# Linear attention and a gated MLP on one core: products from raw turned x with centred weights, queries token by token

## The chip, the cores and the metric

The kernel runs on one NeuronCore of a Trainium2 chip. The metric is device microseconds of one execution. The core has five engines, each with a queue of its own that it works through in order: TensorE (PE in the profile; its weight loads are shown as PEld), VectorE (DVE), ScalarE (ACT), GpSimd (POOL) and SyncE (SP), which here does nothing but issue DMAs. [...]

## The reference

A pre-norm layer on x of 2048 tokens by 448, in bfloat16: linear attention of 16 heads of 28 with softmax feature maps, then an MLP with a gate.

```python
def _layernorm(x): return (x - mean(x)) / sqrt(var(x) + 1e-5)

def _A_ref(x, wqkv, w_phi, wo):
    q, k, v = split((x @ wqkv), heads=16)             # 28 each
    pq, pk = q @ w_phi[h], k @ w_phi[h]
    phi_q = concat([softmax(pq), softmax(-pq)])       # 56 features
    phi_k = concat([softmax(pk), softmax(-pk)])
    kv = einsum("bhsf,bhsd->bhfd", phi_k, v)
    z  = sum over s of phi_k
    o  = (phi_q @ kv) / (phi_q . z + 1e-6)
    return o @ wo

def _B_ref(x, w_gate, w_up, w_down):
    return (sigmoid(x @ w_gate) * (x @ w_up)) @ w_down

h  = x + _A_ref(_layernorm(x), ...)
h2 = h + _B_ref(_layernorm(h), ...)
```

## The kernel before

Tokens are worked in 16 tiles of 128 (t = 0 to 15), in four chunks of 512 (c = 0 to 3). A contraction over 448 rows is done in seven steps of 64 rows, two of them at a time on the upper and lower half of TensorE's array (`pair`, `both`; all such matmuls have the helper's line, L311). The names below are those of the program's operations; each engine's order of them is written out by hand in `ORDER`, and `Graph.emit` adds semaphore waits where one operation needs another's data or buffer. `PROGRAM` lists the stages behind the key and value stage.

Start: x, key, value and query weights are loaded (`x0`.., `ld_k`, `ld_v`, `ld_q`; `ld_q` are transposing DMAs). `w_phi` is spread into block-diagonal form (`wsp`, `wex`), the key weights are turned on TensorE (`wT0` to `wT3`, copied by `wTe`), and key and query weights are multiplied with it (`fold`: `w2m0_k` for the keys, `w2m1_k` for the queries, copied by `w2e`), so that pk and pq are one product from normalized x. `warm0` to `warm9` are matmuls of zeros between these steps. Meanwhile VectorE takes mean and variance of each tile (`bst`, `agg`), GpSimd the power -1/2 (`pow1`), and `xn` writes normalized x. Tiles 0 to 3 are turned on TensorE (`xT0` to `xT3`, `xTe`), tiles 4 to 15 by transposing DMAs (`xT4` to `xT15`, L585) that SP issues as each `xn` is done.

Keys and values, per tile: `ppa/ppb` and `vva/vvb` (two tiles at a time, first four tiles) or `pva/pvb` make pk and v in PSUM; ScalarE takes exp of pk and of -pk (`ek`, L673 and L674) and copies v (`v1`); VectorE sums the exponentials per head (`ss`, L677) and inverts (`rs`); GpSimd or VectorE multiplies (`phi`, L687); TensorE adds phi-transposed times v onto the state in PSUM banks 6 and 7 (`kva`, `kvb`). The state is masked to its heads' blocks in four pieces (`kvzA` to `kvzD`).

Queries, per chunk and half of the heads (`pqa`, `pqb`; eight pairs): the folded query weights are the stationary operand, normalized x the moving one of 512 columns, so pq comes out turned, features on partitions. ScalarE takes exp of it and of its negative (`eq`, L723). These stand as they are for the numerators (`num`, per tile), for which VectorE does the divisions (`rsm qq b c rden`); `o` normalizes, then `oT` turns the result (tiles 0 and 1 on TensorE, others by DMA, L825), `woa/wob` project it. `h` adds x, `sq nm ve pow2` give the second layer norm's numbers, `hn` normalizes, `hT` turns it (tiles 0 and 1 on TensorE, others by DMA, L861). Then per 128 hidden rows `ga/gb` make gate and up, `sig` and `hh` combine them, `dn/dp/dm` project down, `fin` adds and `out` stores.

Of the kernel before, what the change touches and what calls it, by code (L numbers as in the profile page):

```python
# [1021 lines left out]
```

## Time and profile before

| | before |
|---|---|
| median of 3 runs | 204.06 us (203.86 to 204.12) |
| the profiled execution | 203.73 us |
| its span, first to last instruction | 201.9 us |
| busy: PE, DVE, ACT, POOL | 196.3, 132.3, 92.5, 56.5 us |
| DMA moved | 16.27 MB, 32491 packets |
| HBM read, written | 8.34 MB, 1.84 MB |

A row of a group of instructions gives line, engine, operation, what it writes and reads by the program's names, shape and count, then the group's busy time in us and the mean of one in ns, then the engine's idle time before them with what ended it. A row of the timeline or of the chain begins with start and length in us. SPq is SP's sequencer issuing a DMA. A row with x and a slashed triple gives the shortest, middle and longest of one in ns.

### The profile page before, as it was taken

Reading aid. Unit: us, or ns where it says so; the run is one execution under the profiler, and the core shown is the slowest. Engines: PE = TensorE matmul, PEld = TensorE weight load, DVE = VectorE, ACT = ScalarE, POOL = GpSimd, SP = SyncE. Lnnn points to the kernel's source line nnn. Section 1 sums busy time; section 2 is a strip of 40 time slices with the busy share of each in tenths; the row PEclk is TensorE's granted clock in tenths of the full one; section 3 lists DMA queues with packets and bytes.
Section 4 is the critical chain, followed back from the end, with each engine's and each line's share of the span. In section 5 each row is a group of like instructions: output and inputs, shape, how many; then the busy total and the mean of one; then the engine's idle time right before and its main releaser. Section 6 shows DMA issues by size and latency. Waiting matters only on the chain.

```text
span 201.9 us, 5885 instructions
## 1 busy us (share of the span) xinstructions
PE 196.3 (97%) x2516; PEld 114.0 (56%) x2516; DVE 132.3 (65%) x319; ACT 92.5 (46%) x191; POOL 56.5 (28%) x95
## 2 busy tenths in 40 slices
PE   7999999999989999999999999999999999999995
PEld 4835656665558778676444444555555555554443
DVE  4899999978899677767758977436432422272224
ACT  3768998899772636222333342324422212222220
POOL 6579949533433613600042020001400000000000
PEclk9999999999999999999999999999999999999999
DMA  6956444839983320251005411030312000004002
GB/s 155 281 133 159 67 83 78 246 132 269 317 197 75 65 43 3 52 81 29 0 3 123 81 26 26 4 74 28 66 38 52 0 3 0 0 3 136 0 3 91
DMA packets 32491, 16.27 MB, mean 81 GB/s; under 512 B 24720, under 2 KB 31568, under 8 KB 32464
## 3 DMA queue, kind: packets, MB, share of 16 engines
q1 hardware_dynamic: 32336, 15.86, 32.4%
q8 instruction: 20, 0.33, 0.7%
q14 instruction: 7, 0.06, 0.1%
q10 hardware_dynamic: 128, 0.03, 0.1%
HBM read 8.34 MB, written 1.84 MB: 50 GB/s over the span
## 4 chain that ended last, share of the span: by engine, by line
PE 91%; DVE 4%; DMA 2%; SPq 1%; issue 1%; POOL 1%
PE psum L311 84%; PE psum L943 5%; DMA x_sb<-in_A_x_dram 2%; SPq L415 1%; DVE st L547 1%; PE psum L540 1%; DVE st L831 1%; POOL rst L835 1%; PE psum L614 0%; DVE hn_pad L853 0%; DVE xnT L533 0%; DVE b_sb L803 0%; DVE Wk L533 0%; DVE c_sb L806 0%; DVE rsm L800 0%
## 5 line engine op out<-in xcount | busy, mean ns | idle before, releaser
L311 PE MATMUL psum<-xnT,wg_sb 64*128 64x512 bf16 (+1 forms) x490 | 93.1, 333 | 0.2
L311 PE MATMUL psum<-xnT,wu_sb 64*128 64x512 bf16 (+1 forms) x490 | 92.9, 333 | 0.0
L915 ACT ACTIVATE sg_sb<-psum 128x512 bf16<-128x512 f32 (+1 forms) x70 | 34.8, 511 | 91.3 <-PE psum L311 90.8
L916 DVE SCALAR_TENSOR_TENSOR hhT<-sg_sb,psum 128x512 bf16<-128x512 bf16 (+1 forms) x70 | 38.9, 576 | 54.4 <-ACT sg_sb L915 54.2
L311 PEld LDWEIGHTS psum<-xnT,wg_sb 64*128 64x128 bf16 x490 | 44.4, 94 | 22.5 <-DVE hhT L916 4.2
L311 PEld LDWEIGHTS psum<-xnT,wu_sb 64*128 64x128 bf16 x490 | 44.4, 94 | 13.0
L311 PE MATMUL psum<-wd_sb,hhT 64*128 64x448 bf16 x336 | 36.9, 349 | 0.0
L311 PEld LDWEIGHTS psum<-wd_sb,hhT 64*128 64x128 bf16 x336 | 17.6, 94 | 14.4 <-DVE x_sb L838 0.5
L311 PE MATMUL psum<-wv_sb,xnT 64*128 64x448 bf16 x112 | 22.3, 351 | 0.1
L311 PE MATMUL psum<-Wk,xnT 64*128 64x448 bf16 x112 | 22.1, 350 | 0.2
L847 POOL TENSOR_SCALAR ve<-ssq 128x1 f32<-128x1 f32 x11 | 2.2, 201 | 55.0 <-ACT junk L844 54.8
L677 DVE TENSOR_REDUCE ss<-hhT 128x32 f32<-128x896 bf16 x16 | 16.6, 1052 | 0.3 <-ACT hhT L674 0.2
L723 ACT ACTIVATE eq<-psum 120x1024 bf16<-120x1024 f32 x16 | 15.7, 1024 | 1.0 <-PE psum L311 0.8
L687 POOL TENSOR_TENSOR phi<-hhT,rs 128x896 bf16<-128x896 bf16 x8 | 13.7, 1718 | 6.0 <-DVE rs L683 3.6
L311 PE MATMUL psum<-xnT,Wq 64*120 64x512 bf16 x112 | 15.0, 384 | 0.1
L812 POOL TENSOR_TENSOR o_pad<-c_sb,rden 128x448 bf16<-128x448 bf16 x10 | 9.3, 935 | 14.9 <-DVE rden L808 14.8
L311 PE MATMUL psum<-wo_o,oT 64*128 64x448 bf16 x56 | 13.2, 349 | 0.0
L311 PE MATMUL psum<-wo_e,oT 64*128 64x448 bf16 x56 | 13.1, 349 | 0.0
L943 PE MATMUL psum<-wd_sb,hhT 128*128 128x448 bf16 (+2 forms) x70 | 11.2, 316 | 0.0
L950 DVE SCALAR_TENSOR_TENSOR x_sb<-psum,x_sb 128x448 bf16<-128x448 f32 (+2 forms) x17 | 9.4, 592 | 2.7 <-PE psum L943 1.6
L311 PEld LDWEIGHTS psum<-Wk,xnT 64*128 64x128 bf16 x112 | 7.7, 94 | 5.6 <-PE psum L311 1.0
L803 DVE TENSOR_TENSOR b_sb<-psum,qq 128x464 bf16<-128x464 f32 x16 | 10.2, 636 | 0.7 <-PE psum L311 0.4
(105 smaller groups left out, 235.6 us busy)
## 6 DMA issues: line engine op xcount, KB each, us to landing
out_dram<-x_sb SPq DMA_DIRECT2D x15, 112.0 KB, 1.8
x_sb<-in_A_x_dram SPq DMA_DIRECT2D x7, 224.0 KB, 4.0
wd_sb<-in_B_w_down_dram SPq DMA_DIRECT2D x7, 224.0 KB, 4.5
wg_sb<-in_B_w_gate_dram SPq DMA_DIRECT2D x3, 448.0 KB, 6.3
wu_sb<-in_B_w_up_dram SPq DMA_DIRECT2D x3, 448.0 KB, 6.2
wv_sb<-in_A_wqkv_dram SPq DMA_DIRECT2D x2, 224.0 KB, 4.0
wk_sb<-in_A_wqkv_dram SPq DMA_DIRECT2D x2, 196.0 KB, 3.3
wo_e<-in_A_wo_dram SPq DMA_DIRECT2D x1, 336.0 KB, 3.3
```

The source lines that it names most:

```text
L311: p = e.matmul(o, lhsT=w, rhs=r, start=st, stop=sp, tile_position=(row, 0))
L415: return op(eng, name, lambda e: e.dma_start(dst, src), r=r, w=w, dma="in" if eng == "sp" else "ain", nring=48 if eng == "sp" else 8, kb=kb)
L677: op("dve", "ss%d" % t, lambda e: e.tensor_reduce(ss[:, s, :].rearrange("p (b h) -> p b h", h=2), eks.rearrange("p b (d h) -> p b h d", h= ...
L687: return e.tensor_tensor(phi[:, sp, :, :, :].rearrange("p b a n -> p (b a) n")[:, :, 0:56].rearrange("p b (d h) -> p b d h", h=2), eks.rea ...
L723: op("act", "eq%d_%d%s" % (c, i, "pm"[sg]), lambda e, sg=sg: e.activation(eq[c][:, sg, 2 * i:2 * i + 2, :].rearrange("p g n -> p (g n)"), ...
L803: op("dve", "b%d" % t, lambda e: e.tensor_tensor(h3(b_sb), OMv[:, :, :, 0:EV], h2(qq)[:, :, :, None].to_broadcast([P, NB, 8, EV]), ALU.mul ...
L812: return e.tensor_tensor(o_pad[:, t % NO, off:off + D].rearrange("p (h d) -> p h d", h=H), c_sb[:, t % NS, :, 0:DH], rden[:, t % NS, :][:, ...
L847: op(("pool", "dve"), "ve%d" % t, lambda e: e.tensor_scalar(ve2[:, t:t + 1], ssq2[:, t:t + 1], 1.0 / D ** 3, EPS, op0=ALU.mult, op1=ALU.ad ...
L915: op("act", "sig" + nm, lambda e: e.activation(sg_sb[:, k, 0:N], bk(bg)[:, 0:N], ACT.Tanh, scale=0.5), r=[B(bg)], w=[("sg", k)])
L916: op("dve", "hh" + nm, lambda e: e.scalar_tensor_tensor(out=hhT[(t0 // 4) % NHH][:, ff, ns], in0=sg_sb[:, k, 0:N], scalar=1.0, in1=bk(bu)[ ...
L943: p = e.matmul(bk(b)[:, lo:hi], lhsT=hb[:, ff, TS(t)], rhs=wd_sb[:, ff, lo:hi], start=ff == 0, stop=ff == FT - 1)
L950: op("dve", "fin%d%s" % (t, nm), lambda e: e.scalar_tensor_tensor(out=h_sb[:, t, lo:hi], in0=bk(b)[:, lo:hi], scalar=0.5, in1=h_sb[:, t, l ...
```

## The change

Products are made from x as it is loaded. For the mean, the weights are centred: the mean over the 448 rows is taken out of the value weights (`vms` sums by ones on TensorE, `vme` scales, `vc0` and `vc2` add) and of the folded query weights (`qms qme qc0 qc2`); for the keys it is got from a column of ones in the turning matmuls (`identk`, `ksum`, `kmean`) and added by four more matmuls per block (`w2c0` to `w2c3`). The deviation is put in as the scale of the exponentials (`rst1`, and `nrst1` for the negative) and of the `v1` copies. `xn` and the query half of the old layout go. Tiles 0 to 3 of raw x are turned on TensorE (`rT0` to `rT3`), the others two at a time by a transposing DMA of eight 128x128 blocks (`rT4` to `rT14`), for which x is loaded in two overlapping windows (`x_pad`).

Queries are made per tile like keys (448 columns, tokens on partitions, `pqa`, `pqb` for two tiles), their exponentials (`eq0` to `eq15`) go into one of five buffers `eqs`, and one transposing DMA of 16 blocks per two tiles (`eT0` to `eT14`) turns them. Four of the five buffers lie in the MLP's `hhT`, so some `hh` wait for an `eT`. The state's mask is two operations on all partitions (`kvzA`, `kvzB`). h lies where weights lay. All five orders are written anew.

```diff
 ORDER sp:
-x1 x0 ld_k0 ld_k2 x2 x4 ld_v2 x8 x6 ld_q2 ld_q1 ld_v0 x10 ld_q0 ld_q3 xT4 x12 x14 xT5 ... xT15 ld_woe0 ld_woe1
-ld_woo0 ld_woo1 ld_wg0 ld_wu0 ... ld_wu3 ld_wd0 ld_wd1 ld_wd2 oT2 oT3 ld_wd3 ... ld_wd6 oT4 oT5 oT6 oT7 hT2 hT3 oT8 ...
+ld_k2 ld_k0 x0 x4a x4b ld_v2 x1 x2 ld_v0 x6a x6b x10a x10b ld_q2 rT4 ld_q0 ld_q1 ld_q3 ld_woo0 rT8 ld_woe0
+ld_woe1 rT6 ld_woo1 ld_wg3 ld_wd6 ld_wd0 rT10 ld_wd1 ld_wu2 rT12 rT14 ld_wu3 ld_wg2 ld_wd4 ld_wg0 ld_wu1 eT0
+ld_wd3 ld_wu0 eT2 eT4 ld_wg1 eT6 ld_wd5 eT8 oT3 oT2 ld_wd2 eT12 oT4 oT5 oT6 oT7 eT10 hT2 hT3 hT4 eT14 hT5 oT8 ...
 ORDER pe (the start, and from the end of the state on):
-warm0 warm1 warm2 wsp warm3 wT0 wT1 warm4 wT2 wT3 warm5 w2m0_0 w2m0_1 w2m0_2 warm6 w2m0_3 xT1 xT0 warm7 warm8 warm9 xT3 ppa0 ...
+warm0 wsp wT3 wT0 wT2 wT1 warm1 rT1 rT0 w2m0_2 w2m0_3 w2m0_1 w2c2 w2c3 w2c1 rT2 w2m0_0 w2c0 vms rT3 ppa0 ppb0 vva0 ...
-kva15 kvb15 qs pqa1_1 num0 pqb1_1 num1 pqa2_0 num2 pqb2_0 pqa2_1 oT0 oT1 num3 pqb2_1 woa0 wob0 num4 pqa3_0 pqb3_0 wgu
-pqa3_1 num5 pqb3_1 hT1 hT0 num6 ga0_1 ga0_0 gb0_1 gb0_0 woa2 num7 ga0_2 ga0_3 gb0_2 gb0_3 wob2 num8 ga0_4 ga0_5 ... woa4 ...
+kva15 kvb15 qs pqa6 num0 num1 pqb6 pqa8 pqb8 num2 pqa10 oT0 oT1 pqb10 num3 woa0 pqa12 wob0 pqb12 num4 pqa14 pqb14 hT0 hT1
+num5 ga0_1 ga0_0 gb0_1 gb0_0 num6 woa2 ga0_2 ga0_3 gb0_2 wob2 gb0_3 ga0_4 num7 gb0_4 ga0_5 gb0_5 woa4 ...
 ORDER dve:
-... xn0 ... xn2 ... xn11 ... xn12 ... xn14 ...; phi1 3 5 6 11 12 14 15; ... b4 c4 hn0 hn1 rsm5 qq5 b5 hT1e c5 hT0e ...
+... agg3 vc0 vc2 nr1_0 bst7 bst9 agg7 agg2 ss0 ...; phi5 6 9 14 15; ... b4 hn0 hn1 c4 hT0e hT1e rsm5 ...
 ORDER act:
+... v1_10 ek10 eq0 ek11 v1_11 ek12 v1_12 eq1 ek13 ek14 v1_14 ek15 v1_15 eq2 eq3 eq4 ... eq8 oT1e eq9 ... eq12 h0 h1 eq14 eq13 eq15 sig0_1
...
-        def xnorm(t, a): ...
+        def raw(t):
+            if t < NV2:
+                pe_transpose("rT%d" % t, [x_sb[:, t, r0:r0 + P] for r0 in ROW0], 6 + t % 2, xrT[t], ("x", t), ("xr", t))
+            elif t % 2 == 0:
+                dst = hnT[t // 4][:, t % 4:t % 4 + 2, :].rearrange("p t n -> p (t n)").rearrange("p (k n) -> p k n", n=P)
+                src = x_pad[:, t - NV2:t - NV2 + 2, :].rearrange("p t n -> p (t n)")
+                op("sp", "rT%d" % t, lambda e: e.dma_start_transpose(out=dst, in_=src), ...)
...
+        op("dve", "ksum", ... tensor_reduce of the ones' columns ..., r=[B(i) for i in range(6)] + [("WkT", k) for k in range(KT)])
+        def centre(nm, w, key, b, j):
+            def mean(e):
+                for i, (k, h) in enumerate(((0, slice(0, P)), (1, slice(0, P)), (2, HI), (3, slice(0, P)))):
+                    p = e.matmul(bk(b)[:, 0:D], lhsT=ones[h, :], rhs=w[h, k, :], start=i == 0, stop=i == 3)
+                return p
+            op("pe", nm + "ms", mean, ...)
+            op(("act", "dve"), nm + "me", ... mul by -1.0 / D into junk ...)
+            for k in (0, 2):
+                op(("dve", "pool"), "%sc%d" % (nm, k), lambda e, k=k: e.tensor_tensor(w[:, k:k + 2, :], w[:, k:k + 2, :],
+                                                     junk[:, j, None, :].to_broadcast([P, 2, D]), ALU.add), ...)
...
             def ekf(e):
-                e.activation(ek[:, s, :, 0, :], src, ACT.Exp)
-                return e.activation(ek[:, s, :, 1, :], src, ACT.Exp, scale=-1.0)
+                e.activation(ek[:, s, :, 0, :], src, ACT.Exp, scale=rst1[:, t:t + 1])
+                return e.activation(ek[:, s, :, 1, :], src, ACT.Exp, scale=nrst1[:, t:t + 1])
...
         def pq(c, i, b):
-            f1, f2 = pair(bk(b)[:GR, :], bk(b + 1)[:GR, :], lambda h, k: W2[1][h, k, 2 * i, 0:GR], ..., lambda h, k: xnT[c][h, k, :], ...)
-            for sg in range(2):
-                op("act", "eq%d_%d%s" % (c, i, "pm"[sg]), ... Exp of 120x1024, scale=1.0 - 2.0 * sg ...)
+            t = 4 * c + 2 * i
+            proj2("pq", t, b, wq2, W2q)
+            s = eq_at[t // 2]
+            for u in (t, t + 1):
+                def eqf(e, u=u):
+                    src = bk(b + u % 2)[:, 0:D].rearrange("p (b d) -> p b d", b=8)
+                    e.activation(eqs[s][:, u % 2, :, 0, 0:56], src, ACT.Exp, scale=rst1[:, u:u + 1])
+                    return e.activation(eqs[s][:, u % 2, :, 1, 0:56], src, ACT.Exp, scale=nrst1[:, u:u + 1])
+                op("act", "eq%d" % u, eqf, r=[B(b + u % 2), ("rst1", u), ("nrst1", u)], w=[("es", s)])
+            op("sp", "eT%d" % t, lambda e: e.dma_start_transpose(out=eqT[t // 2][:].rearrange("p t b n -> p (t b) n"),
+                                                                 in_=eqs[s].rearrange("p t b a d -> p (t b a d)")),
+               r=[("es", s)], w=[("eqT", t // 2)], dma="tr", nring=64, kb=512)
...
             op("dve", "hh" + nm, ...,
-               w=[("hh", (t0 // 4) % NHH, ff, t % 4) for t in range(t0, t0 + n)])
+               w=[("hh", (t0 // 4) % NHH, ff, t % 4) for t in range(t0, t0 + n)]
+               + [("es", i) for i, lim in enumerate(((8, 13), (10, 14), (6, 10), (2, 6))) if (t0 // 4) % NHH == (i == 0) and lim[0] <= ff < lim[1]])
```

More of the change, by code (lines that the diff above doesn't have):

```diff
@@ L343, in build @@
         ident = sb("ident", [P, P])
+        identk = sb("identk", [GP, GP + 1])
+        ones = sb("ones", [P, P])
         zero = sb("zero", [P, 512])
@@ L368, in build @@
         wv_sb = sb("wv_sb", [P, KT, D])
+        ksum = sb("ksum", [GP, 4], f32)
+        kmean = sb("kmean", [GP, 4])
         WT = [sb("WkT", [GP, KT, D]), sb("WqT", [P, KT, D])]
-        W2 = [sb("Wk2", [P, KT, D]), sb("Wq2", [P, KT, G, P])]
+        W2 = [sb("Wk2", [P, KT, D]), sb("Wq2", [P, KT, D])]
         Wphi = sb("Wphi", [GP, G, GP])
@@ L397, in build @@
         sg_sb = sb("sg_sb", [P, NSG, 512])
+        h_sb = ([W2[0][:, k, :] for k in range(KT)] + [wv_sb[:, k, :] for k in range(KT)] + [WT[1][:, k, :] for k in range(KT)]
+                + [W2[1][:, k, :] for k in range(KT)])
+        h_free = [[("W2", 0, k)] for k in range(KT)] + [[("wv", k)] for k in range(KT)] + [[("WqT", k)] for k in range(KT)] \
+            + [[("W2", 1, k)] for k in range(KT)]
         psum = es.enter_context(nc.psum_tensor("psum", [P, 8 * 512], f32))
@@ L407, in TS, with xt, like @@
             return slice((t % 4) * P, (t % 4 + 1) * P)
+        def xt(t):
+            return x_sb[:, t, :] if t < NV2 else halves(x_pad[:, t - NV2, :])
+        def like(ap, t):
+            return ap if t < NV2 else ap.rearrange("p (a n) -> p a n", a=2)
         g = Graph()
@@ L469, in xload @@
         def xload(a, b):
-            return load("x%d" % a, x_sb[:, a:b, :], x_t[:, a:b, :], [("x", t) for t in range(a, b)], (b - a) * 112)
+            if b <= NV2:
+                load("x%d" % a, x_sb[:, a:b, :], x_t[:, a:b, :], [("x", t) for t in range(a, b)], (b - a) * 112)
+            else:
+                for i, c in enumerate((0, 192)):
+                    load("x%d%s" % (a, "ab"[i]), x_pad[:, a - NV2:b - NV2, 256 * i:256 * i + 256], x_t[:, a:b, c:c + 256],
+                         [("x", t, i) for t in range(a, b)], (b - a) * 64)
         def kload(a, b):
@@ L589, in build @@
+        for t in range(NT):
+            raw(t)
+        for ts in ([0, 1], [2, 3], [4, 5], [6, 7], [8, 9, 10, 11], [12, 13, 14, 15]):
             for t in ts:
@@ L600, in tr @@
                 for gg in range(G):
-                    p = e.transpose(bk16(b)[:GP, gg * GP:(gg + 1) * GP], wk_sb[:, kt, gg * GP:(gg + 1) * GP], ident[:GP, :GP])
+                    p = e.matmul(bk(b)[:GP, gg * (GP + 1):(gg + 1) * (GP + 1)], lhsT=wk_sb[:, kt, gg * GP:(gg + 1) * GP], rhs=identk[:],
+                                 start=True, stop=True)
                 return p
-            op("pe", "wT%d" % kt, tr, r=["ident", ("wk", kt)], w=[B(b)])
+            op("pe", "wT%d" % kt, tr, r=["identk", ("wk", kt)], w=[B(b)])
@@ L604, in build @@
             evac("wTe%d" % kt, WT[0][:, :, kt * GP:(kt + 1) * GP],
-                 bk16(b)[:GP, 0:D].rearrange("p (g i) -> p g i", g=G), B(b), ("WkT", kt))
+                 bk(b)[:GP, 0:G * (GP + 1)].rearrange("p (g i) -> p g i", g=G)[:, :, 0:GP], B(b), ("WkT", kt))
+        op("dve", "ksum", lambda e: e.tensor_reduce(
+            ksum[:], psum[:GP, :].rearrange("p (a c n) -> p a c n", a=2, c=4)[:, :, 0:2, 0:G * (GP + 1)]
+            .rearrange("p a c (g i) -> p g a c i", g=G)[:, :, :, :, GP], AX.XY, ALU.add), r=[B(i) for i in range(6)] + [("WkT", k) for k in range(KT)],
+           w=["ksum"])
@@ new lines, in build @@
+        op(("dve", "pool", "act"), "kmean", (lambda e: e.tensor_scalar(kmean[:], ksum[:], -1.0 / D, None, op0=ALU.mult),) * 2
+           + (lambda e: e.mul(kmean[:], ksum[:], -1.0 / D),), r=["ksum"], w=["kmean"])
+        def centre(nm, w, key, b, j):
[3 more added lines that the diff above has]
+                return p
+            op("pe", nm + "ms", mean, r=["ones"] + [key(k) for k in range(KT)], w=[B(b)])
+            op(("act", "dve"), nm + "me", (lambda e: e.mul(junk[:, j, :], bk(b)[:, 0:D], -1.0 / D),
+                                           lambda e: e.tensor_scalar(junk[:, j, :], bk(b)[:, 0:D], -1.0 / D, None, op0=ALU.mult)),
+               r=[B(b)], w=[("junk", j)])
+            for k in (0, 2):
+                op(("dve", "pool"), "%sc%d" % (nm, k), lambda e, k=k: e.tensor_tensor(w[:, k:k + 2, :], w[:, k:k + 2, :],
+                                                                                     junk[:, j, None, :].to_broadcast([P, 2, D]), ALU.add),
+                   r=[("junk", j), key(k), key(k + 1)], w=[key(k), key(k + 1)])
@@ L607, in fold @@
+        centre("v", wv_sb, lambda k: ("wv", k), 2, 0)
         def fold(w, banks):
@@ L640, in x @@
         def x(t):
-            return lambda h, k: xnT[t // 4][h, k, TS(t)]
+            return lambda h, k: xrT[t][h, k, :]
         def wk2(h, k):
```

226 lines of the change are left out of this document (102 added, 124 removed), and 111 rows, old and new, of the table ORDER.

## The prediction

> **What bounds the kernel now.** I read the engines' shares first, then the busy time by stage, then the chain that ended last, and then the groups inside the two stages that the change touches.
>
> ```profile
> PE 196.3 (97%) x2516; PEld 114.0 (56%) x2516; DVE 132.3 (65%) x319; ACT 92.5 (46%) x191; POOL 56.5 (28%) x95
> PE 91%; DVE 4%; DMA 2%; SPq 1%; issue 1%; POOL 1%
> 16.89:43.90 27.01, 26.79 (x476) 16.56 (x472) 25.78 (x54) 24.26 (x54) 19.31 (x17) 1.00 0.50 120
> 43.90:59.40 15.50, 14.25 (x264) 8.15 (x257) 13.54 (x38) 13.67 (x19) 4.76 (x6) 1.00 0.93 243
> 59.40:78.00 18.60, 18.55 (x326) 14.50 (x328) 15.23 (x48) 8.51 (x25) 7.42 (x13) 1.00 0.30 68
> 78.00:182.00 104.00, 103.90 (x1181) 56.79 (x1176) 57.99 (x136) 32.43 (x69) 13.17 (x27) 1.00 0.16 34
> 12.86:43.30 30.44, 29.81 (x60) 1.00 0.51 126
> ```
>
> The columns of a stage are its length, then the busy us of PE, PE's weight loads, VectorE, ScalarE and GpSimd, the granted clock, DMA share and GB/s; the last row has VectorE alone. TensorE is at 97% and carries 91% of the chain, which looks like one bound from end to end. It is three. From 59.4 us on TensorE leaves nothing idle and no other engine is near it: what arrives late at 59.4 is late at the end, since nothing behind can absorb it. From 12.9 to 43.3 us (keys, values, their softmax) VectorE is busy 29.81 of 30.44 us, so it sets the pace and TensorE's matmuls are stretched between its results. From 43.9 to 59.4 us four engines hand a chain to one another:
>
> ```profile
> 44.40 0.81 DVE L752 TENSOR_TENSOR kvz<-psum,mask 64x232 bf16<-64x232 f32 x2 [1.14 <-PE psum L311]
> 44.40 1.22 ACT L756 ACTIVATE kvz<-psum,mask 64x116 bf16<-64x116 f32 x4
> 56.27 0.73 DVE hn_pad L853 x2
> 57.00 0.18 DVE rsm L800
> 57.21 0.18 DVE qq L801
> 57.41 0.64 DVE b_sb L803
> 58.05 0.33 DVE xnT L533
> 58.38 0.56 DVE c_sb L806
> 58.99 0.40 PE psum L311 x16
> 59.41 9.60 PE psum L311 x172
> L723 ACT ACTIVATE eq<-psum 120x1024 bf16<-120x1024 f32 x16 | 15.7, 1024 | 1.0 <-PE psum L311 0.8
> ```
>
> The state's mask, the first numerators, output projection, second layer norm and its transposes follow one another, and the first gate matmul starts at 59.41 us. The query projections fill TensorE's waits there.
>
> **Query columns: 0 (down to -1.9 us).**
>
> ```profile
> L311 PE MATMUL psum<-xnT,Wq 64*120 64x512 bf16 x112 | 15.0, 384 | 0.1
> L311 PE MATMUL psum<-Wk,xnT 64*128 64x448 bf16 x112 | 22.1, 350 | 0.2
> ```
>
> The 112 query matmuls go from the 512-column to the 448-column form. Two run at once on the array's halves, so 56 x (384 - 350) ns = 1.9 us less of TensorE. Three of the eight pairs lie in VectorE's stage, five in the chain's; both hide them. The added `qms` (four 448-column matmuls, at most 4 x 350 ns) lies in VectorE's stage too; were that cover gone, it would cost 1.4 us.
>
> **The start and the VectorE stage: +0.5 us (-0.3 to +1.2).**
>
> ```profile
> 3.00:5.60 2.60, 2.60 (x23) 2.12 (x22) 1.37 (x5) 0.20 (x1) 1.69 (x5) 1.00 0.93 249
> 3.82 1.70 PE L493 MATMUL psum<-wph,zsel 112*112 112x112 bf16 x16
> 5.53 0.64 PE L601 MATMUL psum<-ident,wk_sb 112*112 112x112 bf16 x8
> 6.00 1.44 ACT L533 COPY WkT<-psum 112x448 bf16<-112x448 bf16 x3 [1.57 <-PE psum L601]
> 6.82 0.81 PE L614 MATMUL psum<-Wphi,WkT 112*128 112x112 bf16 x12
> 10.07 1.74 PE L311 MATMUL psum<-Wk,xnT 64*128 64x448 bf16 x14
> L677 DVE TENSOR_REDUCE ss<-hhT 128x32 f32<-128x896 bf16 x16 | 16.6, 1052 | 0.3 <-ACT hhT L674 0.2
> L687 DVE TENSOR_TENSOR phi<-hhT,rs 128x896 bf16<-128x896 bf16 x8 | 4.6, 598 | 0.0
> L547 DVE BATCH_NORM_STATS2 st<-x_sb 128x6 f32<-128x448 bf16 x7 | 4.1, 614 | 0.0
> L575 DVE TENSOR_SCALAR xn_pad<-x_sb,mv,rst 128x512 bf16<-128x512 bf16 x3 | 1.3, 419 | 0.4 <-issue 0.4
> L673 ACT ACTIVATE hhT<-psum 128x448 bf16<-128x448 f32 x16 | 8.8, 551 | 3.8 <-PE psum L311 3.6
> ```
>
> Raw x needs no statistics before it is turned. But `ksum` reads all four banks of the turned key weights, so every fold now waits for it. The spread matrix ends at 5.5 us, two turns of 0.64 end at 6.8, the third copy (1.44/3) at 7.4, and `ksum` with `kmean` near 8.0 (no row shows them; 0.2 us each, as the `rsm` row above, to 0.55, a copy's). Twelve fold and twelve mean matmuls at 0.81 us each end at 9.6; the last fold and its mean stand behind `rT2` and end near 10.5, and the last copy (551 ns, ScalarE's activation of that size) at 11.1. So the first key projection starts a microsecond later than the 10.07 us of before. Values follow: `vms` (four 448-column matmuls, half of a projection's seven pairs or 0.8 us) from 10.5 to 11.3, `vme` (551 ns) to 11.8, `vc0` and `vc2` (598 ns each, the 128x896 multiply being their nearest row) to 13.0 us, where VectorE's stage begins.
>
> In that stage VectorE loses three of eight `phi` (now GpSimd's) and the three `xn`: -1.8 -1.3 us. It gains three statistics moved behind `vc2` (+1.8), their aggregates, `qc2`, a pad and two negations (about 1.5). The stage keeps its 30.6 us and ends 0.3 us later; GpSimd, with eleven `phi` and its last four close together, adds 0.2: the state is complete near 44.4 us, not 43.9. If ScalarE and VectorE pass the weights on sooner than the queues suggest it is -0.3, if each of them costs a quarter of a microsecond more, +1.2. Exponentials and `v1` copies take the deviation as a scale per partition; so do the four `kvz` on ScalarE (1.22/4 us for 116 columns), so I add nothing, and ScalarE's idle 2.7 us in 16.9 to 43.9 would cover 0.05 us on each. Weight and x loads come in another order, with two overlapping 512-byte pieces for each 896-byte row of twelve x tiles; SP issues thirteen of them ahead of its first transpose. The six `rT` (eight blocks, 2.0 us of SP each by the split below) wait for no statistics; the tightest, `rT6`, stands behind four `WqT`, two others and three loads of `wo`, lands near 21 us and is wanted near 22. A microsecond too late would be one more for VectorE's stage, inside the +1.2.
>
> **The chain: -0.7 us (-1.7 to +0.3).** Two 128-partition `kvz` on VectorE (0.81 us for the present two of half the partitions) replace two there beside four on ScalarE that take 1.22: -0.4. VectorE's queue puts `hT0e hT1e` straight behind `hn0 hn1 c4`; of the rows above `rsm`, `qq`, `b_sb` and `c_sb` between `hn` and the last turn go behind, `c4` comes in: about -0.9. `pqa12` now stands between `woa0` and `wob0`: four 448-column steps, against a bank wait that it hides, +0.5. ScalarE stands at `oT1e` with exponentials queued behind: +0.1. Exponentials: 32 of 551 ns replace 16 of 1024, no change. Gates would start near 59.2 us.
>
> **The exponentials' transposes: +3.4 us (0 to +9.9).** This is the term that decides. SP's queue gets eight `eT`, each of 16 blocks of 128x128, where every transpose so far has four.
>
> ```profile
> 0.72 0.87 SPq L415 DMA_DIRECT2D x_sb<-in_A_x_dram  x2
> 2.60 0.93 SPq L415 DMA_DIRECT2D x_sb<-in_A_x_dram  x2
> L505 SPq DMA_TRANSPOSE WqT<-in_A_wqkv_dram x4: 1134/1226/1252, 5.0 to 9.9; - x4
> L861 SPq DMA_TRANSPOSE xnT<-hn_pad x14: 1189/1227/1932, 69.1 to 151.3; - x14
> DMA to landing us min/median/max: 2.4/2.5/4.3
> 52.32 3.14 SPq L825 DMA_TRANSPOSE oT<-o_pad  x2
> 40.30 0.98 ACT L533 CAST v<-psum 128x448 bf16<-128x448 f32 x2
> 60.94 0.35 PE L311 MATMUL psum<-wo_e,oT 64*128 64x448 bf16 x1
> 65.98 0.35 PE L311 MATMUL psum<-wo_e,oT 64*128 64x448 bf16 x1
> ```
>
> A plain load holds SP for 0.46 us (0.93/2), a four-block transpose for 1.2 us, and it lands 1.3 us after SP lets go of it. How long SP is held for 16 blocks, call it T, no row shows. If the time does not grow with size T is 1.2 us, if all of it does, 4.8. I take a load's 0.46 fixed and the 0.75 above it per four blocks: T = 3.5 us. The nearest rows lean that way: seven eighths of a full turn (`WqT`, 448 rows) reach 1134 ns, the full one never less than 1189.
>
> Now the queue. `eT2` waits for `eq3`, which ScalarE reaches after its last `v1` (41.3 us, and 0.5 late) and four exponentials: 44.0 us. Behind it SP issues `eT4`, a load, `eT6`, a load, `eT8`, then `oT3` and `oT2`, another load, `eT12`, `oT4`, `oT5`. `oT2` therefore lands at 44.0 + 4T + 2 x 0.5 + 2 x 1.2 + 1.3 = 48.7 + 4T = 62.7 us. TensorE wants it for `woa2`, at 60.94 us before, and in the new order at 61.0 (gates 0.2 earlier, `num6` moved ahead 0.3 us): it stands 1.7 us. `oT5` lands a load, an `eT12` and two turns later, at 51.6 + 5T = 69.1; TensorE reaches `woa4` 4.7 us after `woa2` (5.04 between the last two rows, less one `num`, which the row at 58.99 has at 0.40), at 67.4: 1.7 us more. `woa6` and the second chunk's `hT` come in time. TensorE executes in order, so all gate matmuls wait behind these two, and on VectorE `hh0_2` waits for `eT8` besides. With T = 1.2 neither wait exists, with 4.8 they are 6.9 and 3.0 us. That the numerators wait at `num2` for `eT2` is covered by `o0` and `o1` on GpSimd.
>
> [...] No run so far shows a large turn.
>
> **Sum.** +0.5 - 0.7 + 3.4 = +3.2 us. The profiled execution took 203.73 us (span 201.9 and 1.8 around it), 0.33 below the median of the runs, 204.06; 206.9 for it corresponds to 207.3 us at the median.
>
> **The rivals.** (1) *SP's time hardly grows with the size* (T below 2.8 us, where 51.6 + 5T meets the 65.7 us at which an undelayed TensorE comes to `woa4`). For it: two loads of x of double size hold SP for 0.93 us where two single ones took 0.87. Against it: the two transposes' minima above. Then no `oT` is late and start and chain decide: with 0 for the start and -1.2 for the chain (their better halves) 202.9 us, faster; with the values taken, 203.9, no change. (2) *All of a transpose's time grows*: T = 4.8, 9.9 us of waits, 213.8 us. Against it: it would leave no fixed part, and a plain load has one. (3) *A slow start*: the filler matmuls `warm2` to `warm9` go. The rows above have 16 matmuls of 112 columns in 1.70 us at 3.8 us and twelve in 0.81 us at 6.8 (106 and 67 ns each), so the array sped up between. If with fewer matmuls that switch comes only with the dense projections, some 2 us of start work takes 58% longer and the first dense ones too: +2 us on (1), 206 us. Against it: the granted clock is 1.00 in every stage shown, that from 3.0 to 5.6 us included, and the early matmuls that switched it remain. [...]
>
> **Chances.** Forecast 0.46, (1) 0.32, (2) 0.11, (3) 0.11. About 0.2% (0.4 us) is what a measurement of this kernel can tell from no change. Of (1) 0.25 is faster and 0.07 within it; the other cases are all slower, 0.68. Range: down to 202.5, a little past the end of (1); up to 212.5, which leaves out (2) and some of the faster half's tail. The forecast's own range is 205.5 to 210.8 (T from 3.2 to 4.2).
>
> **What would show it.** Right: SP held about 3.5 us by each `eT`; `oT2` issued after 60 us (52.3 before); TensorE idle about 3.5 us in two pieces between 60 and 70 us, released by the DMA of `oT`; the state complete at 44 to 45 us, gates from 59 us; from 70 us on the same matmuls, shifted. The step on T is wrong if `eT` holds SP under 2.8 us; the step on the start, if `vc2` ends before 12.3 us or VectorE is idle there; the whole, if the waits lie behind 78 us.

## The result, and the profile after

The changed kernel takes 214.37 us (median of 4 runs, 213.31 to 216.23) where the kernel before, run beside it, takes 203.96 (203.56 to 204.12): ratio 1.0523, interval 1.0449 to 1.0598. That is 10.4 us slower, with the sign of the forecast and beyond its range. The profiled execution took 214.34 us, span 212.6.

The page of the changed kernel, its engines and the shares of its chain:

```profile
PE 199.2 (94%) x2510; PEld 112.3 (53%) x2510; DVE 136.9 (64%) x331; ACT 98.5 (46%) x200; POOL 52.5 (25%) x79
PE 66%; SPq 9%; DMA 8%; ACT 7%; issue 4%; POOL 2%; DVE 1%; DVEq 0%; POOLq 0%
```

TensorE had carried 91% of the chain; now more than a quarter of it is SyncE, DMA, ScalarE and issue. The stages, cut in both kernels at the same events (first product into the state, last one, first gate matmul, last gate matmul of the first tiles, last output projection); columns as in the prediction. Before:

```profile
16.90:44.18 27.28, 27.00 (x484) 16.67 (x482) 25.77 (x54) 24.53 (x54) 19.30 (x17) 1.00 0.49 119
44.18:59.41 15.23, 14.03 (x256) 8.05 (x254) 13.55 (x38) 13.40 (x19) 4.76 (x6) 1.00 0.94 247
59.41:93.75 34.34, 34.30 (x592) 26.30 (x593) 26.59 (x83) 13.32 (x40) 12.84 (x22) 1.00 0.31 61
93.75:139.80 46.05, 45.95 (x504) 23.01 (x500) 29.71 (x69) 16.32 (x33) 4.71 (x10) 1.00 0.18 40
```

After:

```profile
18.53:49.75 31.22, 28.27 (x488) 15.85 (x485) 27.29 (x52) 28.34 (x55) 22.75 (x17) 1.00 0.90 217
49.75:64.68 14.93, 12.73 (x242) 6.70 (x241) 13.24 (x38) 13.43 (x26) 3.87 (x5) 1.00 1.08 183
64.68:103.67 38.99, 35.97 (x608) 26.20 (x610) 30.29 (x93) 14.84 (x43) 10.00 (x15) 1.00 0.54 92
103.67:150.00 46.33, 46.07 (x504) 22.22 (x499) 29.44 (x72) 15.57 (x31) 5.08 (x10) 1.00 0.21 40
```

So the account of the 10.6 us by which the end moved is: the state's first product 1.6 later (18.53 against 16.90), the state stage 3.9 longer, the chain to the gates 0.3 shorter, the first gates 4.7 longer, and 0.7 behind them. In the state stage ScalarE is busy 28.34 us where it had 24.53. Its groups in the changed kernel:

```profile
L709 ACT ACTIVATE hhT<-psum,rst 128x448 bf16<-128x448 f32 x16 | 10.4, 650 | 2.5 <-PE psum L315 2.3
L710 ACT ACTIVATE hhT<-psum,nrst 128x448 bf16<-128x448 f32 x16 | 10.4, 652 | 0.0
L699 ACT ACTIVATE v<-psum,rst 128x448 bf16<-128x448 f32 x15 | 9.5, 653 | 0.1
```

The same activation without `rst` took 551 ns. The transposes of the exponentials, by tile (shortest, middle, longest ns that one holds SP; then us to landing), and SP's timeline around the third output projection:

```profile
L765 SPq DMA_TRANSPOSE eqT<-hhT x6: 1394/2797/3259, 42.4 to 76.3; - x6
L765 SPq DMA_TRANSPOSE eqT<-eqx x2: 1393/1670/1946, 52.5 to 84.7; - x2
DMA to landing us min/median/max: 4.3/5.2/6.2
```

```profile
62.34 3.65 SPq L864 DMA_TRANSPOSE oT<-o_pad  x2
66.04 0.59 SPq L434 DMA_DIRECT2D wd_sb<-in_B_w_down_dram  x1
66.67 2.78 SPq L765 DMA_TRANSPOSE eqT<-hhT  x1
69.49 6.79 SPq L864 DMA_TRANSPOSE oT<-o_pad  x4
76.32 1.39 SPq L765 DMA_TRANSPOSE eqT<-hhT  x1
```

Two of the eight `eT`, those issued last (76.32 and 84.67), hold SP for 1.39 us each; the other six hold it for 1.8 to 3.3 us. `oT4` goes out at 69.49, behind `eT12`. The chain of the changed kernel shows what this does, and the one late transpose of x:

```profile
20.17 4.81 DMA xnT<-x_pad
29.25 2.31 POOL Wq L639
31.56 2.69 issue
40.28 0.53 ACT hhT L710
40.80 0.53 ACT v L699
63.65 3.59 DMA oT<-o_pad
72.69 2.14 issue
```

TensorE waits for `rT6` until 24.98. From 27.5 to 35.6 the chain runs through `qms`, its copy on ScalarE, `qc0` on GpSimd (the row at 29.25) and the power that GpSimd takes behind it. From 35.6 to 49.4 the chain is nearly all ScalarE's operations back to back, 0.52 to 0.53 us each (two of them above). From 72.69 to 74.84 TensorE stands at the third output projection (`woa4`), whose `oT` are late (`oT5` lands at 74.75); the program's order puts every gate matmul behind that.

### The profile page after: what moved, and what is told of

It reads as the page before. It is cut to its first block, busy times and chain, and to the rows that moved or that the text cites. A ratio compares the mean times of both kernels' runs of the same rounds, so it can differ in the third digit from the quotient of the medians.

```text
span 212.6 us, 5914 instructions
## 1 busy us (share of the span) xinstructions
PE 199.2 (94%) x2510; PEld 112.3 (53%) x2510; DVE 136.9 (64%) x331; ACT 98.5 (46%) x200; POOL 52.5 (25%) x79
## 4 chain that ended last, share of the span: by engine, by line
PE 66%; SPq 9%; DMA 8%; ACT 7%; issue 4%; POOL 2%; DVE 1%; DVEq 0%; POOLq 0%
PE psum L315 61%; PE psum L983 5%; SPq L434 4%; SPq L538 3%; DMA eqT<-hhT 2%; DMA xnT<-x_pad 2%; DMA xnT<-hn_pad 2%; DMA oT<-o_pad 2%; SPq L600 1%; ACT hhT L763 1%; ACT hhT L709 1%; ACT hhT L710 1%; ACT hhT L762 1%; POOL Wq L639 1%; ACT v L699 1%
## 5 line engine op out<-in xcount | busy, mean ns | idle before, releaser
L315 PE MATMUL psum<-xnT,wg_sb 64*128 64x512 bf16 (+1 forms) x490 | 95.7, 334 | 1.7 <-ACT hhT L763 0.8
L315 PE MATMUL psum<-xnT,wu_sb 64*128 64x512 bf16 (+1 forms) x490 | 95.7, 334 | 0.1
L955 DVE SCALAR_TENSOR_TENSOR hhT<-sg_sb,psum 128x512 bf16<-128x512 bf16 (+1 forms) x70 | 40.3, 579 | 54.5 <-ACT sg_sb L954 53.2
L315 PEld LDWEIGHTS psum<-xnT,wg_sb 64*128 64x128 bf16 x490 | 43.7, 94 | 25.6 <-DVE hhT L955 5.3
L723 POOL TENSOR_TENSOR phi<-hhT,rs 128x896 bf16<-128x896 bf16 x11 | 18.9, 1722 | 3.0 <-DVE rs L719 2.1
L713 DVE TENSOR_REDUCE ss<-hhT 128x32 f32<-128x896 bf16 x16 | 16.9, 1066 | 1.2 <-ACT hhT L710 1.0
L888 POOL TENSOR_TENSOR rst<-ve,neghalf 128x1 f32<-128x1 f32 x14 | 8.1, 584 | 25.8 <-DVE ve L886 21.7
L851 POOL TENSOR_TENSOR o_pad<-c_sb,rden 128x448 bf16<-128x448 bf16 x7 | 6.5, 935 | 27.2 <-DVE rden L847 27.2
L315 PE MATMUL psum<-Wq,xnT 64*128 64x448 bf16 x112 | 13.0, 349 | 0.1
L709 ACT ACTIVATE hhT<-psum,rst 128x448 bf16<-128x448 f32 x16 | 10.4, 650 | 2.5 <-PE psum L315 2.3
L710 ACT ACTIVATE hhT<-psum,nrst 128x448 bf16<-128x448 f32 x16 | 10.4, 652 | 0.0
```

Source lines behind the costliest of these rows:

```text
L315: p = e.matmul(o, lhsT=w, rhs=r, start=st, stop=sp, tile_position=(row, 0))
L709: e.activation(ek[:, s, :, 0, :], src, ACT.Exp, scale=rst1[:, t:t + 1])
L710: return e.activation(ek[:, s, :, 1, :], src, ACT.Exp, scale=nrst1[:, t:t + 1])
L713: op("dve", "ss%d" % t, lambda e: e.tensor_reduce(ss[:, s, :].rearrange("p (b h) -> p b h", h=2), eks.rearrange("p b (d h) -> p b h d", h= ...
L723: return e.tensor_tensor(phi[:, sp, :, :, :].rearrange("p b a n -> p (b a) n")[:, :, 0:56].rearrange("p b (d h) -> p b d h", h=2), eks.rea ...
L851: return e.tensor_tensor(o_pad[:, t % NO, off:off + D].rearrange("p (h d) -> p h d", h=H), c_sb[:, t % NS, :, 0:DH], rden[:, t % NS, :][:, ...
```

## The experiments

All times are medians; "state" is the start of the last product into the state and "gates" that of the first gate matmul, from the timeline of each profiled run. Each ratio is to the kernel before as run beside that kernel, 203.84 to 204.00 us.

| kernel | us | ratio to before, interval | state | gates |
|---|---|---|---|---|
| before | 203.96 | | 44.18 | 59.41 |
| after | 214.37 | 1.0523 (1.0449 to 1.0598) | 49.75 | 64.68 |
| before_scaled | 206.42 | 1.0135 (1.0095 to 1.0176) | 46.21 | 61.44 |
| const_scale | 214.24 | 1.0494 (1.0444 to 1.0545) | 48.92 | 62.90 |
| rT6_first | 214.21 | 1.0515 (1.0487 to 1.0543) | 48.89 | 63.69 |
| oT_first | 211.91 | 1.0406 (1.0376 to 1.0435) | 49.27 | 64.07 |
| eT_split | 213.66 | 1.0483 (1.0460 to 1.0506) | 49.56 | 64.50 |
| queues_mended | 210.88 | 1.0353 (1.0316 to 1.0391) | 49.21 | 64.00 |
| queues_const | 209.49 | 1.0272 (1.0243 to 1.0301) | 46.59 | 60.88 |
| few_transposes | 208.20 | 1.0201 (1.0181 to 1.0220) | 47.29 | 61.62 |
| no_centring | 207.65 | 1.0176 (1.0160 to 1.0193) | 46.58 | 60.59 |
| both_left_out | 207.02 | 1.0144 (1.0124 to 1.0163) | 46.32 | 61.04 |
| before_early_copies | 205.56 | 1.0076 (1.0059 to 1.0093) | 44.94 | 59.62 |

**The price of the scale by itself: before_scaled.**

```diff
-e.activation(ek[:, s, :, 0, :], src, ACT.Exp)
-return e.activation(ek[:, s, :, 1, :], src, ACT.Exp, scale=-1.0)
+e.activation(ek[:, s, :, 0, :], src, ACT.Exp, scale=uno[:, 0:1])      # a column of 1
+return e.activation(ek[:, s, :, 1, :], src, ACT.Exp, scale=uno[:, 1:2])  # of -1; v1 likewise
```

> The kernel before, with a per-partition scale of +1 and -1 on the key exponentials and of +1 on the v1 copies; the results stay the same. Theory A: 45 of ScalarE's operations in the state stage cost 0.1 us more, 4.5 us in all, against 2.7 us of idle time that ScalarE has there, so the last state matmul comes 1 to 3 us later than 44.18 and the time is 205 to 207 us. Theory B (the prediction's own step, cover for the price): 203.9 to 204.3 us.

Two of its groups, and then its state stage:

```profile
L682 ACT ACTIVATE hhT<-psum,uno 128x448 bf16<-128x448 f32 x16 | 10.4, 649 | 0.0
L681 ACT ACTIVATE hhT<-psum,uno 128x448 bf16<-128x448 f32 x16 | 10.4, 649 | 2.9 <-PE psum L311 2.8
```

```profile
17.34:46.21 28.87, 27.37 (x484) 16.74 (x482) 26.12 (x52) 27.35 (x54) 19.06 (x17) 1.00 0.49 110
```

Each exponential goes from 551 to 649 ns though the factors are 1 and -1: it was the operand that cost, 98 ns each, not the value. ScalarE's 2.7 idle us take up part of the 45 x 0.1, the state comes 2.03 us later, the gates 2.03, the kernel 2.6. Theory A holds.

**The same price taken out of the changed kernel: const_scale.**

```diff
-e.activation(ek[:, s, :, 0, :], src, ACT.Exp, scale=rst1[:, t:t + 1])
+e.activation(ek[:, s, :, 0, :], src, ACT.Exp, scale=1.0)      # ek, eq and v1 alike
```

> The changed kernel, with the per-partition scale of the key and query exponentials replaced by the constants +1 and -1 and the v1 copies made plain; the deviation is left out of the computation, everything else and every wait stays. Theory A (the scale per partition is a price on ScalarE: 650 ns an exponential where the kernel before shows 551, and ScalarE is the chain from 26.9 to 49.4 us): some 38 ScalarE operations lie in that stretch, 0.095 us each, so the last state matmul comes 3 to 3.6 us earlier than 49.75 and the time is 210.5 to 211.5 us. Theory B (the key stage is longer because of late transposes and of the order in ScalarE's queue, the price lies beside other work): the exponentials take 551 ns, the last state matmul stays within 0.7 us of 49.75 and the time is 213.5 to 214.4 us.

The exponentials are back at 556 ns, but the state comes only 0.8 us earlier, the gates 1.8, and the time stays. Two things took the gain in the profiled execution. In the state stage the chain changes hands: in place of ScalarE's it now holds VectorE's and GpSimd's `phi` and sums, and TensorE still waits 1.6 us for `rT6`.

```profile
30.45 1.81 DVE phi L723
32.26 1.99 DVE ss L713 x2
37.77 1.70 POOL phi L723
```

And at the third output projection TensorE's granted clock fell. These are the stretches of equal length after TensorE's stand there, in const_scale (first) and in the changed kernel:

```profile
73.06:76.00 2.94, 2.94 (x23) 1.89 (x25) 0.29 (x2) 0.00 (x0) 0.00 (x0) 0.50 0.31 59
```

```profile
74.84:77.78 2.94, 2.94 (x42) 2.21 (x42) 0.65 (x4) 0.38 (x1) 0.00 (x0) 1.00 0.31 60
```

TensorE stood idle for 2.14 us in both. In const_scale the granted clock is 0.50 afterwards, and 23 matmuls run where 42 do. From that projection's first matmul to the last gate of the first tiles it takes 30.33 us (73.06 to 103.39) against 28.83 (74.84 to 103.67): between the two profiled executions the clock costs 1.5 us. For the medians this is not shown. The one run of const_scale at a mean clock of 1.00 took 212.33 us, the three at 0.992 213.97 to 214.86; but the changed kernel has such runs too, 214.34 at 1.00, 213.31 and 214.40 at 0.992, 216.23 at 0.984. At 1.00 const_scale is 2.0 us faster (one run each), at 0.992 it is not faster. So this run alone decides nothing between the theories.

**The order of SyncE's queue: rT6_first and oT_first.**

```diff
-ld_woo0 rT8 ld_woe0 ld_woe1 rT6 ld_woo1
+ld_woo0 rT6 ld_woe0 ld_woe1 rT8 ld_woo1
```

> The changed kernel, with the transposes of tiles 6, 7 and of tiles 8, 9 exchanged in SyncE's queue. Theory A (the order of SyncE's queue makes the start late): tiles 6, 7 land near 22.4 us where they landed at 24.98, TensorE's wait of 1.58 us is gone, and 1.0 to 1.6 us of it are still there at the end, 212.7 to 213.4 us. Rival (ScalarE is late anyway and takes up the gain, or tiles 8, 9 are then late by as much): the wait goes, the time is within 0.4 us of 214.3.

The wait for `rT6` is gone; the state comes 0.9 us earlier and the gates 1.0, then TensorE stands idle for 2.29 us at `woa4` and the half clock follows here too (30.32 us from there to the last gate). The time is unchanged, as the rival said. In the profiled execution it was the half clock that took the gain. All four runs have a mean clock of 0.992 and took 213.82 to 215.11 us, and the changed kernel's two at that clock were no slower; so at an equal clock no gain is left either, and what took it there no trace shows.

```diff
-eT6 ld_wd5 eT8 oT3 oT2 ld_wd2 eT12 oT4 oT5 oT6 oT7 eT10
+eT6 ld_wd5 oT3 oT2 eT8 ld_wd2 oT4 oT5 eT12 oT6 oT7 eT10
```

> The changed kernel, with the output transposes oT3 and oT2 moved ahead of the exponentials' transpose eT8 in SyncE's queue, and oT4 and oT5 ahead of eT12. Theory A (an output transpose stands behind a 16-block one, and TensorE stands for it): the stands at the third and second wo step, 0.4 and 2.3 us, go, the gates of the first tiles end 1.5 to 2.7 us earlier, 211.7 to 212.8 us. Rival (the same transposes in another order only move the stand to eT8's readers, the gate combine that overwrites its source among them): within 0.4 us of 214.3.

```profile
64.07:100.36 36.29, 35.76 (x608) 25.75 (x610) 30.27 (x93) 14.85 (x43) 10.00 (x15) 1.00 0.74 109
```

The first gates take 36.29 us (38.99), with no wait for an `oT` left, and the kernel is 2.5 us faster (at a mean clock of 1.00, 211.29 and 211.34 us against 214.34). That the output transposes stood behind 16-block ones is shown.

**What a transpose holds SP: eT_split.**

```diff
-dma_start_transpose(out=eqT[i] /* 16 blocks */, in_=eqs[s])
+for u in range(2): dma_start_transpose(out=eqT[i][:, u] /* 8 blocks */, in_=eqs[s][:, u])
```

> The changed kernel with each 16-block transpose of the exponentials issued as two 8-block ones in the same place of SyncE's queue; same data, same packets. Theory A (what a transpose holds SyncE is some 1.3 us an instruction whatever its blocks, and more only where the transfers ahead of it have not drained): the two halves hold SyncE 1.3 us each where one alone held 1.39 (eT10, eT14), and together about as long as the whole one did, 2.8 to 3.3 us, where the queue is full; first halves land sooner; 213.5 to 216.5 us. Theory B (the prediction's T: the hold grows with the blocks): each half holds half as long as a whole one, 0.7 us for eT10 and eT14, and the time stays within 0.5 us of 214.3.

```profile
L766 SPq DMA_TRANSPOSE eqT<-hhT x12: 1242/1345/1922, 42.2 to 78.9; - x12
L766 SPq DMA_TRANSPOSE eqT<-eqx x4: 1318/1327/1337, 52.4 to 86.6; - x4
DMA to landing us min/median/max: 3.1/4.2/5.3
```

A half holds SP for 1.34 us, nearly as long as the whole ones that held it for 1.39; the whole ones of the burst, 2.0 to 3.3 us, held it about as long as two halves do (2.6 to 3.3 us). So theory B falls: the hold did not grow by the block. Theory A is shown in its first part alone. That a longer hold comes from transfers ahead that have not drained does not come out of the rows: in the changed kernel `eT2`, issued at 49.40 when the last transfer ahead had landed at 49.17, held SP for 3.02 us, and `eT10` held it for 1.39 with `oT7` still in flight (landed 77.51). What makes a hold long stays open. Halves land 1 us sooner (4.2 us at the median against 5.2); the time is 0.7 us lower, which its interval (1.0460 to 1.0506 against 1.0449 to 1.0598) does not tell from no change.

**Only places in queues: queues_mended, then with constant scales: queues_const.**

```diff
 sp:    rT6_first and oT_first
-dve:   bst14 qc2 agg13 phi5 ss6 ss7 agg12 agg14 rs6 rs7
+dve:   bst14 agg13 agg12 agg14 qc2 qc0 ss6 ss7 rs6 rs7
-pool:  pow1_8 nr1_8 qc0 pow1_12 phi7
+pool:  pow1_8 nr1_8 phi5 pow1_12 phi7
-act:   w2e1_0 w2e1_1 nr1_4 ek4 v1_4 w2e1_2 v1_5 ek5 w2e1_3 ek6
+act:   nr1_4 ek4 v1_4 w2e1_0 w2e1_1 v1_5 ek5 w2e1_2 w2e1_3 ek6
-pe:    kva0 w2m1_0 w2m1_1 pva4 kvb0 pvb4 pva5 w2m1_3 w2m1_2 pvb5 kva1 pva6
+pe:    kva0 pva4 kvb0 pvb4 w2m1_0 w2m1_1 pva5 pvb5 kva1 w2m1_3 w2m1_2 pva6
```

> The changed kernel with every operation kept and only places in queues changed: the two moves of rT6_first and oT_first together; VectorE's variances of tiles 12 to 15 ahead of phi5 and of two sums, so that GpSimd and then ScalarE no longer stand for them; half of the query weights' centring on VectorE (0.63 us) in place of GpSimd (2.31) and phi5 on GpSimd in place of VectorE; the query fold on TensorE and ScalarE one tile later. Theory A (of the 5.6 us by which the state is late, the greater part beyond the start is made by work that stands in a queue behind other work, and ScalarE's price is only one of several late things there): the last state matmul near 47 us (49.27 in oT_first) and the time 209 to 210.3 us, where oT_first has 211.9. Theory B (ScalarE's price alone sets the stage): the last state matmul stays later than 48.7 us and the time within 0.6 us of 211.9.

> The kernel queues_mended with the per-partition scales of the exponentials and v1 copies replaced by constants, as in const_scale; the deviation is left out of the computation. Theory A (the price of the scale was covered in const_scale by the other late things, and counts once these are gone, as the 2.6 us of before_scaled say): 1.5 to 3 us less than queues_mended, with the last state matmul 1.5 to 2.5 us earlier. Theory B (the price is covered all the same, by VectorE or GpSimd): within 0.6 us of queues_mended.

The state stage of queues_mended, and then that of queues_const:

```profile
18.48:49.21 30.73, 28.00 (x488) 16.04 (x486) 26.12 (x52) 28.22 (x55) 22.24 (x17) 1.00 0.93 224
```

```profile
17.91:46.59 28.68, 27.47 (x488) 15.39 (x486) 25.75 (x52) 24.43 (x56) 21.96 (x17) 1.00 1.02 239
```

With all queues mended and the scales in place the state is as late as in oT_first (49.21 against 49.27): my theory A for queues_mended falls, and ScalarE holds the stage. Its 210.88 us is 1.0 below oT_first, more than theory B allowed; at a mean clock of 1.00 (210.76 to 210.96 against 211.29 and 211.34) 0.5 of it is left. With the scales gone as well, the state comes 2.6 us earlier and the gates 3.1; in the changed kernel with its queues the same edit was worth 0.8 and 1.8. So two limits lay beside each other in the state stage, and each covered the other's removal: ScalarE's price, and the queue places. At the end 1.4 us of the 3.1 are left, just under theory A's 1.5 to 3. The rest is in SyncE's queue and in the chain of queues_const:

```profile
59.95 3.19 SPq L763 DMA_TRANSPOSE eqT<-hhT  x1
63.82 2.50 SPq L862 DMA_TRANSPOSE oT<-o_pad  x2
68.32 1.28 issue
```

TensorE now arrives 3 us sooner and stands for `oT4` and `oT5` again, which wait for SP behind `eT8` and a load. `oT5`, issued at 65.05, also takes 4.45 us to land.

**Fewer transposes, and no centring of keys and values, on queues_const.**

```diff
-op("sp", "eT%d" % t, ...)                       # few_transposes
+t < 8 and op("sp", "eT%d" % t, ...)             # num8.. read eqT of tiles 0 to 7
-w2c0 w2c1 w2c2 w2c3 ksum kmean vms vme vc0 vc2  # no_centring: these operations go
```

> The kernel queues_const without the transposes eT8, eT10, eT12 and eT14; the products with the state of tiles 8 to 15 read the turned exponentials of tiles 0 to 7, so the right data of those tiles is left out. Theory A (SyncE, held 3.0 to 3.2 us by eT8 and by eT12, is what makes the output transposes of tiles 4 and 5 late, and TensorE stands 1.5 us for them at the third wo step): the stand goes and the gates of the first tiles take 35.3 to 36.2 us where they took 37.5; 207.2 to 208.3 us. Rival (the outputs o4 and o5 are themselves late, by VectorE's chain): within 0.4 us of 209.5.

SP's timeline in few_transposes, and its first gates:

```profile
60.70 0.58 SPq L432 DMA_DIRECT2D wd_sb<-in_B_w_down_dram  x1
63.65 8.94 SPq L862 DMA_TRANSPOSE oT<-o_pad  x4
```

```profile
61.62:97.64 36.02, 35.74 (x607) 25.88 (x609) 30.58 (x95) 14.68 (x43) 9.99 (x15) 1.00 0.31 52
```

The stand is gone and the first gates take 36.0 us where they took 37.5; 1.3 us, as theory A had it. SP is free at 61.3 and waits for `o4`, and `oT5` lands 2.49 us after its issue; so the stand was made by the place in the queue and by the longer landing together. In the profiled execution the start was 0.7 us later (first key projection at 12.05 where queues_const has 11.34, with the same program up to there), which hides part: the twelve folds took 1.32 us at 8.39, where queues_const took 0.76 at 8.24.

> The kernel queues_const without the centring of the key and value weights (32 small matmuls, their sums, the mean matmuls, the copy and two additions ahead of the first value projection); the mean is left in. Theory A (the centring makes the start late): the first key projection near 10.0 us where it was at 11.34, and 0.8 to 1.5 us of it are left at the end, 208.0 to 208.7 us. Rival (after the first four tiles the stage waits for the transposed tiles 4 to 7 and for ScalarE anyhow): the first key projection is earlier, the last state matmul within 0.4 us of 46.6 and the time 209.1 us or more.

Two pieces of its chain:

```profile
24.10 1.54 SPq L432
26.25 5.11 DMA xnT<-x_pad
```

The first key projection comes at 10.53 (11.34), but the state not at all earlier (46.58): TensorE then waits until 31.36 for tiles that a transposing DMA turns, and SP issues that one behind a row of loads, of which the one shown held it for 1.54 us. That is the rival's picture. Yet the time falls by 1.8 us, more than either expected; of the 1.4 us between the two profiled spans 0.8 lie in the first gates (36.7 us against 37.5, no stand at `woa4`): here `eT8` held SP for 1.98 us and not 3.19, so `oT4` went out 1.1 us sooner. Why `eT8` held SP for less I can't tell from the traces.

> The kernel queues_const with both left out, eT8 to eT14 as in few_transposes and the key and value centring as in no_centring. If the two are terms of one sum, the time falls by the sum of their two gains, to 206 to 207.2 us, and what is then left over the kernel before, 2 to 3 us, is in the key stage; rival (one covers the other): the time is that of the better of the two, within 0.4 us.

It takes 207.02 us: 2.5 us below queues_const, where the sum of the two gains is 3.1 and the better one 1.8; inside the range that was expected of a sum, though 0.6 short of the full one. Both edits end the same stand at `woa4`, so their gains can add up only in part. What is left over the kernel before, 3.0 us, is not in the key stage alone: it lies in the state stage and the chain behind it (gates at 61.04 against 59.41) and in the gates of the first tiles, 36.0 us against 34.34, among them one `num` more (0.4), which stood ahead of the gates before. These 3 us were not taken apart further.

**A version of the kernel before: before_early_copies.**

```diff
-b5 hT1e c5 hT0e      # dve        hT1 hT0 num6 ga0_1 ga0_0 gb0_1 gb0_0   # pe
+b5 hT1e hT0e c5                   hT1 hT0 ga0_1 ga0_0 gb0_1 gb0_0 num6
```

> The kernel before with VectorE's copies of both turned first tiles (hT1e, hT0e) ahead of the sum c5 and TensorE's product num6 behind the first two gate blocks. TensorE stood 0.95 us there for c5. Theory: the gates start at 58.7 to 58.9 us where they started at 59.41, and 0.4 to 0.7 us stay, 203.3 to 203.6 us. Rival (c5 and what hangs on it, o5 and the third wo step, are then late by as much): 203.8 to 204.2 us.

It is 1.6 us slower, and slower than either expected. A piece of its chain at the first gates, and TensorE's longest wait behind them (us in total, times, longest):

```profile
56.46 3.78 ACT eq L723 x4
PE psum L311 <- DVE c_sb L806: 1.2, 1, 1.2
```

The gates start at 59.62 us, not earlier. In the profiled execution the first key projection is 0.8 us later (10.84 against 10.07) at a start that the edit leaves alone; from the state to the gates it takes 14.68 us for 15.23. The chain runs through ScalarE's last exponentials, to 60.24, ahead of the second gate block, and `num6`, moved behind, then makes VectorE's `b` and `c` late, for which TensorE stands 1.2 us. No kernel here beats the kernel before.

## Why the prediction was right or wrong

The forecast was +3.2 us; between the profiled executions it was +10.6. By its terms: the state is 5.6 us later where 0.5 was forecast, the chain 0.3 shorter (0.7), the first gates 4.7 longer (3.4), and 0.7 came behind them (0).

- **Query columns, 0.** 112 of 349 ns, as forecast; that the saving is hidden fits the stages above, but no run isolates it.
- **Start and VectorE stage, +0.5 (-0.3 to +1.2).** Here the prediction failed: the state was late by 5.6 us (49.75; forecast 44.4). The start came near: `vc2` ends at 13.38 us, where 13.0 was forecast, though the first key projection is 1.7 us later than before and not 1 (leaving the centring out takes 0.8 of it). It is the stage behind that took 5 us more than forecast. The largest piece of it that the runs show is the sentence "so I add nothing, and ScalarE's idle 2.7 us in 16.9 to 43.9 would cover 0.05 us on each". The nearest row that I took for it, a `kvz` of 116 columns, took 354 ns, of which I could not tell the scale's share. The price is 0.10 us on each of some 45 key exponentials and `v1` copies (before_scaled: 2.0 us at the state after the cover is used up) and on the 32 query exponentials. With the queues out of the way it is 2.6 us at the state and 3.1 at the gates (queues_mended to queues_const).
- **`rT6` near 21 us, wanted near 22.** It landed at 24.98 and TensorE waited 1.6 us. The forecast had named this as the tightest one, but not that some issues ahead of it hold SP longer than its rows had shown (a load of x 1.71 us, a `WqT` 2.15 in the chain).
- **The bound of the stage.** I had VectorE set the pace and TensorE's matmuls stretched between its results. The chain of the kernel before (first row below) has TensorE alone for 22.51 us of that stage, so VectorE kept close to the pace and did not set it. In the changed kernel ScalarE sets it, with VectorE, GpSimd and the transposes of x within a microsecond behind: that is why const_scale and rT6_first, each alone, moved the state by less than 1 us and the time not at all. In queues_const (the other rows) TensorE has the pace again, and the state is still 2.4 us later than before:

```profile
20.95 22.51 PE psum L311 x394
26.17 1.07 PE psum L630 x4
30.62 14.38 PE psum L313 x249
```

1.0 of the 2.4 is a later first product (17.91 against 16.90). The row at 26.17 is `qms`, which the forecast had put at nothing under VectorE's cover: with TensorE in the chain its 1.07 us count. That is read from the chain; no run leaves `qms` out.

- **The chain, -0.7.** Right in sign, and -0.3 lies in its range: 14.93 us against 15.23. Its terms were not tested one by one. The last wait ahead of the first gate is for ScalarE's exponentials (0.83 us), for which the forecast had 0.1.
- **The exponentials' transposes, +3.4.** The effect is there, the mechanism is not the one put. T did not grow by blocks: whole ones held SP for 1.39 us at the least, halves for 1.24 (eT_split). The middle values of the two rows whose minima I had compared, 1226 and 1227 ns, had shown no growth either. In the queue ahead of `oT5` the five `eT` hold SP for 13.8 us, 2.8 each and not 3.5. The stands were forecast at `woa2` and `woa4`, 1.7 us each; measured 0.4 and 2.1, ending at 67.38 and 74.84 us, as everything was 5 us late by then. That the size came near is luck: from `eT2`'s issue to `oT5`'s landing are 25.4 us (49.40 to 74.75), where the forecast had 25.1 (51.6 + 5T - 44.0); the `eT` took 3.7 us less of it, and loads, four-block transposes, the gaps between issues and the landing took 3.9 more. Undoing the order gave 2.5 us back (oT_first).
- **Rivals.** Of (1), "SP's time hardly grows with the size" is right for 8 and 16 blocks, and its T, below 2.8 us, is just met; its conclusion, that no `oT` is late, is wrong: some holds were long all the same, and the rest of the queue was slower than forecast. (2) falls. Of (3) more is true than the granted clock tells, which reads 1.00 in the views from the start on. Three rows of TensorE in the changed kernel:

```profile
5.50 1.73 PE L616 MATMUL psum<-identk,wk_sb 112*112 112x113 bf16 x16
8.30 1.13 PE L651 MATMUL psum<-Wphi,WkT 112*128 112x112 bf16 x12
9.27 0.75 PE L660 MATMUL psum<-Wphi,kmean 112*128 112x112 bf16 x12
```

Measured as the forecast did, one takes 108, 94 and 62 ns; before, the folds at 6.82 took 67 already. So the array sped up near 9 us here, where before it had by 6.8. In few_transposes it came later than in queues_const, and the first key projection with it by 0.7 us. No run puts the `warm` matmuls back, so what their absence costs is open. The clock also entered behind the stand at `woa4`, as below.

- **Behind 78 us** nothing of weight was to come; 0.7 us did (0.3 of it up to the last output projection). I did not follow it.

## What to carry to other kernels

A scale that turned from a constant into a per-partition column had a price on each of ScalarE's activations here (551 to 649 ns in before_scaled). For such an operand look for two rows of the same shape and operation that differ in that alone, and if there are none, do not put it at nothing: here it was 0.10 us times all such instructions in the stage. Where several engines are within a microsecond of the pace, take out one late thing after another in combination, since each alone was covered by the next here: const_scale and rT6_first, each alone, moved the state by 0.8 and 0.9 us and the time not at all. And in an engine's queue of DMAs put what a waiting engine needs ahead of what is only large: moving four output transposes ahead of two 16-block ones was worth 2.5 us here.
